# A GELU feed-forward block: all of x through DMA transposes on SyncE's queue, the plain loads on ScalarE's

## The chip, the core and the metric

The kernel runs on one core of a Trainium2 chip. A core has TensorE (PE: matrix products, with its own weight loads), VectorE (DVE), ScalarE (ACT), GpSimd (POOL) and SyncE (SP), which only issues DMAs and waits here. SyncE, ScalarE and GpSimd each have a queue from which DMAs are issued; one set of 16 DMA engines carries them out. The metric is the device time of one execution in microseconds. All times in the text count from the first instruction of the profiled execution.

## What is computed

```python
B, S, D, F = 1, 2048, 448, 1792           # bfloat16
h = jnp.einsum("bsd,df->bsf", x, w1) + b1
h = gelu(h)                               # tanh form
return jnp.einsum("bsf,fd->bsd", h, w2) + b2
```

Both products contract over the leading axis of what sits on the 128 partitions. So the first needs x with D on the partitions, that is x transposed; the second needs h with F on the partitions, which is how the first product writes it.

## The kernel before

**Tiling.** S = 2048 is cut into four chunks of 512 columns (c = 0 to 3). F = 1792 is 14 tiles of 128 (ft). D = 448 is covered by four slots of 128 rows that begin at rows 0, 128, 256 and 320 (k = 0 to 3; slots 2 and 3 overlap by 64 rows). A tile of the first product is therefore three full matmuls and one half, with 64 rows. Halves of neighbouring tiles run side by side.

**Order on TensorE.** Layer 1 of chunks 0 and 1, layer 2 of chunk 0, layer 1 of chunk 2, and so on; the order of the eight PSUM banks is fixed by hand (`jobs`, `number`). A chunk of layer 1 is two blocks: tiles 0 to 7, then 8 to 13. The first block of chunk 0 is written apart (`opening_block`): it runs k = 0 over all eight tiles, then k = 1 over all eight, then waits for k = 2 and 3 of w1 and does the rest. The second block waits for `sem_w1r`, the rest of w1's columns. ScalarE applies bias and GELU to each finished tile (L298), VectorE adds b2 to each output tile (L319), and SyncE stores it.

**The loads before.** SyncE issues all but one, in this order: chunk 0 of x as it lies in memory, in two halves (`xn_sb`, L142 and L143); the four k pieces of w1's first eight column tiles, 256 KB each (L120); the rest of w1's columns in two DMAs, 576 and 192 KB (L121 and L124); chunk 1 of x by four DMA transposes (L134), each of which brings 512 rows by 128 columns, 128 KB; w2 in two pieces of 784 KB (L128); b2 spread over the partitions (L148); chunks 2 and 3 of x by eight DMA transposes. GpSimd loads b1 (L164) after it has made the identity matrix.

**Chunk 0 before.** TensorE first runs NWARM = 11 matmuls on zeros (L170). Then it transposes chunk 0 against the identity (16 matmuls, L178) into PSUM; VectorE copies k = 0 and 1 to `xT_sb` (two casts, L310), ScalarE k = 2 and 3 (two casts, L291). b1 is transposed the same way (L187). The opening block waits for those copies: two of VectorE before the first matmul, b1 before the fourth, ScalarE's before the sixth and eighth.

```python
waits = {0: (sem_xTd, 2), 3: (sem_b1, 1), 5: (sem_xTa, 1), 7: (sem_xTa, 2)}
for k in (0, 1):
    pe.wait_ge(sem_w1[k], 16)
    for n, ft in enumerate(fts):
        if k == 0 and n in waits:
            pe.wait_ge(*waits[n])
        full(0, ft, k, k == 0, False)
```

Because chunk 0 is loaded with four neighbouring rows on one partition, its rows come out in another order, and its stores use a view of the output that puts them back (`out0_view`).

Of the kernel before, what the change touches and what calls it, by code (L numbers as in the profile page):

```python
# [7 lines left out]
BF16 = mybir.dt.bfloat16  # L8
# [3 lines left out]
def bass_standalone__dense_activation_gelu__prompt_kernel(  # L12
# [20 lines left out]

    KROW = [0, 128, 256, 320]
    NKT = len(KROW)

    WCUT = 8 * P
# [5 lines left out]
    W2_PIECES = [(0, 7), (7, 14)]  # L43
    NB = 8

    NWARM = 11
    WN = 256

    OCUT = 256
# [21 lines left out]
    with ExitStack() as es:  # L71
        sb = lambda n, s, d: es.enter_context(nc.sbuf_tensor(n, s, d))
        xT_sb = sb("xT_sb", [P, NKT, S], BF16)
        w1_sb = sb("wi_sb", [P, NKT, F], BF16)
        w2_sb = sb("wo_sb", [P, NFT, D], BF16)
        xn_sb = sb("xn_sb", [P, STC, D], BF16)
# [15 lines left out]
        sem_xn = [S_(f"sem_xn{i}") for i in range(2)]  # L92
# [4 lines left out]
        sem_xtp = S_("sem_xtp")  # L97
        sem_xTd = S_("sem_xTd")
        sem_xTa = S_("sem_xTa")
        sem_b1T = S_("sem_b1T")  # L100
        sem_b1 = S_("sem_b1")
        sem_l1 = S_("sem_l1")
# [4 lines left out]

        block = es.enter_context(nc.Block())


        x0_view = x2[0:SC, :].rearrange("(p t) d -> p t d", t=STC)
        out0_view = out2[0:SC, :].rearrange("(p t) d -> p t d", t=STC)

        def out_dram(j):
            return out0_view[:, j, :] if j < STC else out2[j * P:(j + 1) * P, :]

        def load_w1(eng):
            with nc.allow_non_contiguous_dma(reason="w1 column pieces"):
                for k, r in enumerate(KROW):
                    eng.dma_start(w1_sb[:, k, 0:WCUT], w1[r:r + P, 0:WCUT]).then_inc(sem_w1[k], 16)  # L120
                eng.dma_start(  # L121
                    w1_sb[:, 0:3, WCUT:F], w1[0:3 * P, WCUT:F].rearrange("(k p) f -> p k f", p=P)
                ).then_inc(sem_w1r, 16)
                eng.dma_start(w1_sb[:, 3, WCUT:F], w1[KROW[3]:D, WCUT:F]).then_inc(sem_w1r, 16)  # L124

        def load_w2(eng, i):
            a, b = W2_PIECES[i]
            eng.dma_start(  # L128
                w2_sb[:, a:b, :], w2[a * P:b * P, :].rearrange("(ft p) d -> p ft d", p=P)
            ).then_inc(sem_w2[i], 16)  # L130

        def load_xT(eng, c):
            for k, d0 in enumerate(KROW):
                eng.dma_start(  # L134
                    xT_sb[:, k, c * SC:(c + 1) * SC],
                    x2[c * SC:(c + 1) * SC, d0:d0 + P],
                    transpose=True,
                ).then_inc(sem_x[c], 16)

        @block.sync  # L140
        def _(sp):
            sp.dma_start(xn_sb[:, 0:2, :], x0_view[:, 0:2, :]).then_inc(sem_xn[0], 16)  # L142
            sp.dma_start(xn_sb[:, 2:4, :], x0_view[:, 2:4, :]).then_inc(sem_xn[1], 16)  # L143
            load_w1(sp)
            load_xT(sp, 1)
            for i in range(len(W2_PIECES)):
                load_w2(sp, i)
            sp.dma_start(b2_bc[:, :], b2.partition_broadcast(P)).then_inc(sem_b2, 16)  # L148
            for c in range(2, NSC):
                load_xT(sp, c)  # L150
# [16 lines left out]
        def _(pe):  # L167
            pe.wait_ge(sem_zero, 1)
            for _i in range(NWARM):
                pe.matmul(ps[0][:, 0:WN], lhsT=zeros[:, 0:P], rhs=zeros[:, :], start=True, stop=True)  # L170
            pe.wait_ge(sem_id, 2)

            for h in range(2):
                pe.wait_ge(sem_xn[h], 16)
                for k, d0 in enumerate(KROW):
                    for t in range(2):
                        col = (k % 2) * 2 * P + t * P
                        mm = pe.matmul(  # L178
                            ps[4 + 2 * h + k // 2][:, col:col + P],
                            lhsT=xn_sb[:, 2 * h + t, d0:d0 + P],  # L180
                            rhs=ident[:, :],
                            start=True, stop=True,
                        )
                    if k % 2:
                        mm.then_inc(sem_xtp, 1)
            pe.wait_ge(sem_b1n, 16)
            pe.matmul(  # L187
                ps[3][:, 0:NFT], lhsT=b1n_sb[:, :], rhs=ident[0:NFT, 0:NFT], start=True, stop=True
            ).then_inc(sem_b1T, 1)

            def free(kind, i):
                n = number[kind, i] - NB
                if n >= 0:
# [22 lines left out]
            def opening_block(first, second):  # L216

                fts = first + second
                waits = {0: (sem_xTd, 2), 3: (sem_b1, 1), 5: (sem_xTa, 1), 7: (sem_xTa, 2)}
                for k in (0, 1):  # L220
                    pe.wait_ge(sem_w1[k], 16)
                    for n, ft in enumerate(fts):
                        if k == 0 and n in waits:
                            pe.wait_ge(*waits[n])
                        full(0, ft, k, k == 0, False)
                pe.wait_ge(sem_w1[2], 16)
                pe.wait_ge(sem_w1[3], 16)
                for n, ft in enumerate(first):
                    full(0, ft, SLOTS[n % 2][2], False, False)
                for n, ft in enumerate(first):  # L230
                    half(0, ft, *HALVES[n % 2], False, True).then_inc(sem_l1, 1)
# [52 lines left out]

        @block.scalar
        def _(act):
            act.wait_ge(sem_zero, 1)
            act.activation(act_junk[:, :], zeros[:, 0:8], ACT.Gelu_apprx_tanh)  # L288
            for h in range(2):
# [12 lines left out]
            act.wait_ge(sem_osb, len(outs))  # L302
            act.dma_start(out_dram(NST - 1), out_sb[:, NST - 1, :]).then_inc(sem_od, 16)

        @block.vector
        def _(dve):
            dve.memset(zeros[:, :], 0.0).then_inc(sem_zero, 1)  # L307
            for h in range(2):
                dve.wait_ge(sem_xtp, 2 * h + 1)
                dve.tensor_copy(  # L310
                    xT_sb[:, 0:2, h * 256:(h + 1) * 256],
                    ps[4 + 2 * h][:, :].rearrange("p (k t) -> p k t", k=2),
                ).then_inc(sem_xTd, 1)
            dve.wait_ge(sem_b1T, 1)
            dve.tensor_copy(b1_f[:, :], ps[3][:, 0:NFT]).then_inc(sem_b1, 1)  # L315
# [35 lines left out]
```

## Time and profile before

| | |
|---|---|
| median of three runs | 97.1 us (96.87 to 99.33) |
| the profiled execution | 96.71 us |
| its span, first to last instruction | 94.9 us |
| TensorE busy | 90.8 us, 96% of the span |
| ScalarE busy | 35.8 us, 38% |
| VectorE busy | 11.8 us, 12% |
| first GELU of a real tile (L298) | 10.67 us |
| first store of an output tile (L153) | 31.35 us |
| granted clock of TensorE | 1.000 |

The page gives busy time by engine, the chain of waits that ended last, and the costliest groups of instructions. The DMA issues come with the time from issue to landing:

```profile
wo_sb<-in_w_dram SPq DMA_DIRECT2D x2, 784.0 KB, 7.0
wi_sb<-in_w_dram SPq DMA_DIRECT2D x4, 256.0 KB, 4.7
wi_sb<-in_w_dram SPq DMA_DIRECT2D x1, 576.0 KB, 6.3
xn_sb<-in_x_dram SPq DMA_DIRECT2D x2, 224.0 KB, 2.6
wi_sb<-in_w_dram SPq DMA_DIRECT2D x1, 192.0 KB, 6.3
xT_sb<-in_x_dram SPq DMA_TRANSPOSE x12, 4.4
```

Each line reads: what is written from what, the issuing queue, the operation, how many, the size of one, and the median time to landing in microseconds. `wi_sb` is w1, `wo_sb` is w2. A busy TensorE is not one at its peak, since its matmuls are pipelined and their ends are modelled; where the chain runs along TensorE without a break, the end moves one for one with what starts that stretch.

### The profile page before, as it was taken

What the parts mean: (1) busy time and instruction counts of PE and PEld (TensorE: products, weight loads), DVE (VectorE), ACT (ScalarE), POOL (GpSimd) and SP (SyncE); (2) the same over time, 40 slices, a digit from 0 to 9 for tenths busy, and PEclk for the clock granted to TensorE, in tenths of its full rate; (3) what the DMA queues carried; (4) which work ended last, traced back from release to release, by engine and by line L of the source; (5) the groups of instructions that cost most, each with busy time, mean ns of one, the idle gap of its engine ahead of it and who ended that gap; (6) DMA issues with size and microseconds to landing.
All of it is one profiled execution on the core that took longest, in us unless ns stands there. A gap on an engine that the chain in (4) does not pass through costs nothing.

```text
span 94.9 us, 1157 instructions
## 1 busy us (share of the span) xinstructions
PE 90.8 (96%) x490; PEld 44.1 (46%) x490; DVE 11.8 (12%) x21; ACT 35.8 (38%) x60; POOL 1.3 (1%) x7
## 2 busy tenths in 40 slices
PE   5989999999999999999999999999999999999990
PEld 3744343434345555434445545434435555555670
DVE  0230000000000222200000222200000222222130
ACT  6130599969395000059486000049577000000000
POOL 5000000000000000000000000000000000000000
DMA  2999989997520111100000111010000110111111
GB/s 48 303 289 342 211 204 368 205 111 137 94 52 0 48 48 48 33 22 0 0 3 0 48 48 43 8 52 0 0 0 0 48 42 13 41 48 55 48 48 48
DMA packets 12245, 7.50 MB, mean 79 GB/s; under 512 B 6992, under 2 KB 11728, under 8 KB 12240
## 3 DMA queue, kind: packets, MB, share of 16 engines
q1 hardware_dynamic: 12064, 7.31, 32.4%
q10 hardware_dynamic: 144, 0.11, 0.4%
q8 instruction: 4, 0.07, 0.3%
q0 software_dynamic: 32, 0.00, 0.0%
q14 instruction: 1, 0.01, 0.0%
HBM read 4.02 MB, written 1.84 MB: 62 GB/s over the span
## 4 chain that ended last, share of the span: by engine, by line
PE 95%; DVE 1%; issue 0%
PE ps L274 45%; PE ps L198 39%; PE ps L206 7%; PE ps L170 3%; PE ps L178 1%; DVE xT_sb L310 1%; DVE out_sb L319 0%; DVE zeros L307 0%
## 5 line engine op out<-in xcount | busy, mean ns | idle before, releaser
L298 ACT ACTIVATE g_sb<-ps,bi_f 128x512 bf16<-128x512 f32 x56 | 33.1, 706 | 33.9 <-PE ps L206 33.9
L274 PE MATMUL ps<-wo_sb,g_sb 128*128 128x448 bf16 (+2 forms) x238 | 42.9, 341 | 0.0
L198 PE MATMUL ps<-xT_sb,wi_sb 128*128 128x512 bf16 x168 | 38.1, 379 | 0.4 <-DVE xT_sb L310 0.4
L274 PEld LDWEIGHTS ps<-wo_sb,g_sb 128*128 128x128 bf16 x238 | 23.1, 98 | 19.7
L198 PEld LDWEIGHTS ps<-xT_sb,wi_sb 128*128 128x128 bf16 x168 | 15.7, 98 | 21.5 <-issue 3.4
L319 DVE TENSOR_TENSOR out_sb<-ps,bo_bc 128x448 bf16<-128x448 f32 (+2 forms) x17 | 10.2, 597 | 76.9 <-PE ps L274 76.9
L206 PE MATMUL ps<-xT_sb,wi_sb 64*128 64x512 bf16 x56 | 7.4, 379 | 0.0
L206 PEld LDWEIGHTS ps<-xT_sb,wi_sb 64*128 64x128 bf16 x56 | 2.1, 94 | 4.8 <-issue 3.4
L170 PE MATMUL ps<-zeros 128*128 128x256 bf16 x11 | 2.5, 419 | 1.1 <-DVE zeros L307 1.1
L170 PEld LDWEIGHTS ps<-zeros 128*128 128x128 bf16 x11 | 1.5, 145 | 1.6 <-DVE zeros L307 1.1
L291 ACT CAST xT_sb<-ps 128x512 bf16<-128x512 f32 x2 | 1.2, 585 | 2.4 <-PE ps L178 2.4
L310 DVE CAST xT_sb<-ps 128x512 bf16<-128x512 f32 x2 | 1.4, 692 | 3.2 <-PE ps L178 3.2
L178 PE MATMUL ps<-ident,xn_sb 128*128 128x128 bf16 x16 | 1.8, 300 | 0.0
L178 PEld LDWEIGHTS ps<-ident,xn_sb 128*128 128x128 bf16 x16 | 1.6, 142 | 0.3 <-issue 0.3
L288 ACT ACT_TABLE_LOAD x1 | 1.3, 1283 | 0.7 <-PEq L336 0.7
L164 POOL DMA_DIRECT2D bin_sb<-in_b_dram x1 | 0.6, 647 | 0.2 <-issue 0.2
L160 POOL TENSOR_SCALAR_AFFINE_SELECT ident<-ident 128x128 bf16<-128x128 bf16 x1 | 0.3, 287 | 0.2 <-POOL ident L158 0.2
L307 DVE MEMSET zeros<- 128x128 uint32 x1 | 0.2, 165 | 0.8 <-PEq L336 0.8
L288 ACT ACTIVATE act_junk<-zeros 128x8 bf16<-128x8 bf16 x1 | 0.2, 208 | 0.0
L158 POOL MEMSET ident<- 128x128 bf16 x1 | 0.2, 204 | 0.3 <-POOLq L336 0.3
L187 PE MATMUL ps<-ident,bin_sb 14*128 14x14 bf16 x1 | 0.2, 177 | 0.0
L315 DVE COPY bi_f<-ps 128x14 f32<-128x14 f32 x1 | 0.2, 162 | 0.0
(5 smaller groups left out, 0.5 us busy)
## 6 DMA issues: line engine op xcount, KB each, us to landing
out_dram<-out_sb SPq DMA_DIRECT2D x15, 112.0 KB, 1.7
wo_sb<-in_w_dram SPq DMA_DIRECT2D x2, 784.0 KB, 7.0
wi_sb<-in_w_dram SPq DMA_DIRECT2D x4, 256.0 KB, 4.7
wi_sb<-in_w_dram SPq DMA_DIRECT2D x1, 576.0 KB, 6.3
xn_sb<-in_x_dram SPq DMA_DIRECT2D x2, 224.0 KB, 2.6
wi_sb<-in_w_dram SPq DMA_DIRECT2D x1, 192.0 KB, 6.3
xT_sb<-in_x_dram SPq DMA_TRANSPOSE x12, 4.4
bo_bc<-in_b_dram SPq DMA_DIRECT2D x1, 112.0 KB, 7.6
```

What stands on the lines that cost most here:

```text
L160: pool.affine_select(out=ident[:, :], in_=ident[:, :], compare_op=ALU.not_equal, fill=1.0, base=0, pattern=[[-1, P]], channel_multiplier=1 ...
L164: pool.dma_start(b1n_sb[:, :], b1.rearrange("(c p) -> c p", p=P)).then_inc(sem_b1n, 16)
L170: pe.matmul(ps[0][:, 0:WN], lhsT=zeros[:, 0:P], rhs=zeros[:, :], start=True, stop=True)
L178: mm = pe.matmul(ps[4 + 2 * h + k // 2][:, col:col + P], lhsT=xn_sb[:, 2 * h + t, d0:d0 + P], rhs=ident[:, :], start=True, stop=True,)
L198: return pe.matmul(bank("g", order.index((c, ft)))[:, :], lhsT=w1_sb[:, k, ft * P:(ft + 1) * P], rhs=xT_sb[:, k, c * SC:(c + 1) * SC], sta ...
L206: return pe.matmul(bank("g", order.index((c, ft)))[:, :], lhsT=w1_sb[lo:lo + HALF, k, ft * P:(ft + 1) * P], rhs=xT_sb[lo:lo + HALF, k, c * ...
L274: mm = pe.matmul(bank("o", n)[:, 0:c1 - c0], lhsT=g_sb[:, ft, j * P:(j + 1) * P], rhs=w2_sb[:, ft, c0:c1], start=(ft == 0), stop=(ft == NF ...
L288: act.activation(act_junk[:, :], zeros[:, 0:8], ACT.Gelu_apprx_tanh)
L291: act.copy(xT_sb[:, 2:4, h * 256:(h + 1) * 256], ps[5 + 2 * h][:, :].rearrange("p (k t) -> p k t", k=2),).then_inc(sem_xTa, 1)
L298: act.activation(g_sb[:, ft, c * SC:(c + 1) * SC], bank("g", i)[:, :], ACT.Gelu_apprx_tanh, bias=b1_f[:, ft:ft + 1], scale=1.0,).then_inc( ...
L310: dve.tensor_copy(xT_sb[:, 0:2, h * 256:(h + 1) * 256], ps[4 + 2 * h][:, :].rearrange("p (k t) -> p k t", k=2),).then_inc(sem_xTd, 1)
L319: dve.tensor_tensor(out=out_sb[:, j, c0:c1], in0=bank("o", n)[:, 0:c1 - c0], in1=b2_bc[:, c0:c1], op=ALU.add,).then_inc(sem_osb, 1)
```

## The change

Chunk 0 of x now also comes by four DMA transposes, one per k, each with a semaphore of its own (`sem_x0[k]`). SyncE issues nothing but the sixteen transposes of x, chunk after chunk, and then the stores. ScalarE's queue takes the plain loads, ahead of ScalarE's first activation: the four pieces of w1, its rest, w2 and b2. TensorE's transposes of chunk 0, their four copies, `xn_sb` and the changed row order of chunk 0 go. NWARM is 17. The transposition of b1 stands between the second and the third matmul of the opening block, and its result is awaited before the eighth. The waits for k = 2 and 3 cover both x and w1.

```diff
-    NWARM = 11
+    NWARM = 17
...
+        sem_x0 = [S_(f"sem_x0_{k}") for k in range(NKT)]
...
-        def load_xT(eng, c):
-            for k, d0 in enumerate(KROW):
-                eng.dma_start(
-                    xT_sb[:, k, c * SC:(c + 1) * SC],
-                    x2[c * SC:(c + 1) * SC, d0:d0 + P],
-                    transpose=True,
-                ).then_inc(sem_x[c], 16)
+        def load_xT(eng, c, k):
+            eng.dma_start(
+                xT_sb[:, k, c * SC:(c + 1) * SC],
+                x2[c * SC:(c + 1) * SC, KROW[k]:KROW[k] + P],
+                transpose=True,
+            ).then_inc(sem_x[c] if c else sem_x0[k], 16)
...
         def _(sp):
-            sp.dma_start(xn_sb[:, 0:2, :], x0_view[:, 0:2, :]).then_inc(sem_xn[0], 16)
-            sp.dma_start(xn_sb[:, 2:4, :], x0_view[:, 2:4, :]).then_inc(sem_xn[1], 16)
-            load_w1(sp)
-            load_xT(sp, 1)
-            for i in range(len(W2_PIECES)):
-                load_w2(sp, i)
-            sp.dma_start(b2_bc[:, :], b2.partition_broadcast(P)).then_inc(sem_b2, 16)
-            for c in range(2, NSC):
-                load_xT(sp, c)
+            for c in range(NSC):
+                for k in range(NKT):
+                    load_xT(sp, c, k)
...
                 for k in (0, 1):
+                    pe.wait_ge(sem_x0[k], 16)
                     pe.wait_ge(sem_w1[k], 16)
                     for n, ft in enumerate(fts):
-                        if k == 0 and n in waits:
-                            pe.wait_ge(*waits[n])
+                        if k == 0 and n == 2:
+                            pe.wait_ge(sem_id, 2)
+                            pe.wait_ge(sem_b1n, 16)
+                            pe.matmul(
+                                ps[NB - 1][:, 0:NFT], lhsT=b1n_sb[:, :], rhs=ident[0:NFT, 0:NFT],
+                                start=True, stop=True,
+                            ).then_inc(sem_b1T, 1)
+                        if k == 0 and n == NB - 1:
+                            pe.wait_ge(sem_b1, 1)
                         full(0, ft, k, k == 0, False)
-                pe.wait_ge(sem_w1[2], 16)
-                pe.wait_ge(sem_w1[3], 16)
+                for k in (2, 3):
+                    pe.wait_ge(sem_x0[k], 16)
+                    pe.wait_ge(sem_w1[k], 16)
...
         def _(act):
+            for k in range(NKT):
+                load_w1(act, k)
+            load_w1_rest(act)
+            for i in range(len(W2_PIECES)):
+                load_w2(act, i)
+            act.dma_start(b2_bc[:, :], b2.partition_broadcast(P)).then_inc(sem_b2, 16)
             act.wait_ge(sem_zero, 1)
             act.activation(act_junk[:, :], zeros[:, 0:8], ACT.Gelu_apprx_tanh)
-            for h in range(2):
-                act.wait_ge(sem_xtp, 2 * h + 2)
-                act.copy(
-                    xT_sb[:, 2:4, h * 256:(h + 1) * 256],
-                    ps[5 + 2 * h][:, :].rearrange("p (k t) -> p k t", k=2),
-                ).then_inc(sem_xTa, 1)
```

`load_w1(eng, k)` and `load_w1_rest(eng)` are the two parts of the former `load_w1`, with the same DMAs.

More of the change, by code (lines that the diff above doesn't have):

```diff
@@ L75, in bass_standalone__dense_activation_gelu__prompt_kernel @@
         w2_sb = sb("wo_sb", [P, NFT, D], BF16)
-        xn_sb = sb("xn_sb", [P, STC, D], BF16)
         ident = sb("ident", [P, P], BF16)
@@ L91, in bass_standalone__dense_activation_gelu__prompt_kernel @@
         sem_b2 = S_("sem_b2")
-        sem_xn = [S_(f"sem_xn{i}") for i in range(2)]
+        sem_x0 = [S_(f"sem_x0_{k}") for k in range(NKT)]
         sem_b1n = S_("sem_b1n")
@@ L96, in bass_standalone__dense_activation_gelu__prompt_kernel @@
         sem_id = S_("sem_id")
-        sem_xtp = S_("sem_xtp")
-        sem_xTd = S_("sem_xTd")
-        sem_xTa = S_("sem_xTa")
         sem_b1T = S_("sem_b1T")
@@ L108, in bass_standalone__dense_activation_gelu__prompt_kernel, with load_w1, load_w1_rest @@
         block = es.enter_context(nc.Block())
-        x0_view = x2[0:SC, :].rearrange("(p t) d -> p t d", t=STC)
-        out0_view = out2[0:SC, :].rearrange("(p t) d -> p t d", t=STC)
         def out_dram(j):
-            return out0_view[:, j, :] if j < STC else out2[j * P:(j + 1) * P, :]
-        def load_w1(eng):
+            return out2[j * P:(j + 1) * P, :]
+        def load_w1(eng, k):
             with nc.allow_non_contiguous_dma(reason="w1 column pieces"):
-                for k, r in enumerate(KROW):
-                    eng.dma_start(w1_sb[:, k, 0:WCUT], w1[r:r + P, 0:WCUT]).then_inc(sem_w1[k], 16)
+                eng.dma_start(
+                    w1_sb[:, k, 0:WCUT], w1[KROW[k]:KROW[k] + P, 0:WCUT]
+                ).then_inc(sem_w1[k], 16)
+        def load_w1_rest(eng):
+            with nc.allow_non_contiguous_dma(reason="w1 column pieces"):
                 eng.dma_start(
@@ L130, in load_w2 @@
             ).then_inc(sem_w2[i], 16)
-        def load_xT(eng, c):
-            for k, d0 in enumerate(KROW):
-                eng.dma_start(
-                    xT_sb[:, k, c * SC:(c + 1) * SC],
-                    x2[c * SC:(c + 1) * SC, d0:d0 + P],
-                    transpose=True,
-                ).then_inc(sem_x[c], 16)
+        def load_xT(eng, c, k):
+            eng.dma_start(
+                xT_sb[:, k, c * SC:(c + 1) * SC],
+                x2[c * SC:(c + 1) * SC, KROW[k]:KROW[k] + P],
+                transpose=True,
+            ).then_inc(sem_x[c] if c else sem_x0[k], 16)
         @block.sync
         def _(sp):
-            sp.dma_start(xn_sb[:, 0:2, :], x0_view[:, 0:2, :]).then_inc(sem_xn[0], 16)
-            sp.dma_start(xn_sb[:, 2:4, :], x0_view[:, 2:4, :]).then_inc(sem_xn[1], 16)
-            load_w1(sp)
-            load_xT(sp, 1)
-            for i in range(len(W2_PIECES)):
-                load_w2(sp, i)
-            sp.dma_start(b2_bc[:, :], b2.partition_broadcast(P)).then_inc(sem_b2, 16)
-            for c in range(2, NSC):
-                load_xT(sp, c)
+            for c in range(NSC):
+                for k in range(NKT):
+                    load_xT(sp, c, k)
             for j in range(NST - 1):
@@ L170, in _ @@
                 pe.matmul(ps[0][:, 0:WN], lhsT=zeros[:, 0:P], rhs=zeros[:, :], start=True, stop=True)
-            pe.wait_ge(sem_id, 2)
-            for h in range(2):
[L174 to L189, printed above, removed]
             def free(kind, i):
@@ L218, in opening_block @@
                 fts = first + second
-                waits = {0: (sem_xTd, 2), 3: (sem_b1, 1), 5: (sem_xTa, 1), 7: (sem_xTa, 2)}
                 for k in (0, 1):
+                    pe.wait_ge(sem_x0[k], 16)
                     pe.wait_ge(sem_w1[k], 16)
                     for n, ft in enumerate(fts):
-                        if k == 0 and n in waits:
-                            pe.wait_ge(*waits[n])
+                        if k == 0 and n == 2:
[7 more added lines that the diff above has]
+                            pe.wait_ge(sem_b1, 1)
                         full(0, ft, k, k == 0, False)
-                pe.wait_ge(sem_w1[2], 16)
-                pe.wait_ge(sem_w1[3], 16)
+                for k in (2, 3):
+                    pe.wait_ge(sem_x0[k], 16)
+                    pe.wait_ge(sem_w1[k], 16)
                 for n, ft in enumerate(first):
@@ L286, in _ @@
         def _(act):
+            for k in range(NKT):
[4 more added lines that the diff above has]
+            act.dma_start(b2_bc[:, :], b2.partition_broadcast(P)).then_inc(sem_b2, 16)
             act.wait_ge(sem_zero, 1)
             act.activation(act_junk[:, :], zeros[:, 0:8], ACT.Gelu_apprx_tanh)
-            for h in range(2):
-                act.wait_ge(sem_xtp, 2 * h + 2)
-                act.copy(
-                    xT_sb[:, 2:4, h * 256:(h + 1) * 256],
-                    ps[5 + 2 * h][:, :].rearrange("p (k t) -> p k t", k=2),
-                ).then_inc(sem_xTa, 1)
             act.wait_ge(sem_b1, 1)
@@ L307, in _ @@
             dve.memset(zeros[:, :], 0.0).then_inc(sem_zero, 1)
[L308 to L313, printed above, removed]
             dve.wait_ge(sem_b1T, 1)
-            dve.tensor_copy(b1_f[:, :], ps[3][:, 0:NFT]).then_inc(sem_b1, 1)
+            dve.tensor_copy(b1_f[:, :], ps[NB - 1][:, 0:NFT]).then_inc(sem_b1, 1)
             dve.wait_ge(sem_b2, 16)
```

## Prediction

> **What bounds the kernel now.** I read the chain of waits first, by engine and then in order of time. By engine:
>
> ```profile
> PE 95%; DVE 1%; issue 0%
> ```
>
> TensorE carries the chain; only its start holds anything that is not matrix work. The pieces in order of time (start, length, what) show where a change to the first loads can act:
>
> ```profile
> 1.06 2.53 PE ps L170 x11
> 3.59 1.32 PE ps L178 x12
> ...
> 4.93 0.70 DVE xT_sb L310
> ...
> 5.77 4.48 PE ps L198 x20
> ```
>
> Warm-up matmuls, the transposes of chunk 0, one copy out of PSUM, and at 5.77 us the first real matmul. From there PE runs unbroken to 92.36. So the new time is the old one plus the shift of the last point at which PE waits for data. That point is somewhere in the first blocks of chunk 0, so I read SyncE's own timeline next (start, length of all):
>
> ```profile
> 1.67 1.85 SPq L120 DMA_DIRECT2D wi_sb<-in_w_dram  x4
> 3.56 0.43 SPq L121 DMA_DIRECT2D wi_sb<-in_w_dram  x1
> 4.03 0.49 SPq L124 DMA_DIRECT2D wi_sb<-in_w_dram  x1
> 4.56 5.83 SPq L134 DMA_TRANSPOSE xT_sb<-in_x_dram  x4
> ```
>
> A plain load costs the issuing queue 0.43 to 0.49 us, a DMA transpose about three times that. More important is the order: the transposes of chunk 1 stand behind all of w1. The answer for line L134 between 20.7 and 26 us, where nothing else is queued, gives the bare cost (min/median/max ns, then landing in us from the start of issue):
>
> ```profile
> L134 SPq DMA_TRANSPOSE xT_sb<-in_x_dram x4: 1262/1262/1263, 20.6 to 24.6; - x4
> ...
> DMA to landing us min/median/max: 3.2/3.5/3.6
> ```
>
> With 0.05 between them, one transpose leaves every 1.31 us. The DMA views of two stretches, 3.3 to 8.5 (almost only w1) and 21 to 22 (only transposes), give the two rates:
>
> ```profile
> DMA packets 958, 1.56 MB, mean 301 GB/s; under 512 B 114, under 2 KB 450, under 8 KB 958
> ```
> ```profile
> DMA packets 1036, 0.25 MB, mean 249 GB/s; under 512 B 1036, under 2 KB 1036, under 8 KB 1036
> ```
>
> Two transposes a microsecond: 0.5 us of all 16 engines each, in 512 packets of 256 B, 32 per engine. A 256 KB piece of w1 (128 rows, 8 packets per engine) takes 0.87 us at 301 GB/s, 0.11 a packet. Last, the table by stage around 20 us (PE, PEld, DVE, ACT, POOL, clock, DMA share, GB/s) and, for 18.9 to 20.9, the DMA queues:
>
> ```profile
> 19.40:20.90 1.50, 1.50 (x12) 0.55 (x12) 0.00 (x0) 1.02 (x2) 0.00 (x0) 1.00 1.64 16
> ```
> ```profile
> q1 hardware_dynamic: 560, 0.14, 148.7%
> q8 instruction: 1, 0.02, 3.7%
> ```
>
> Transposes were queued, yet traffic fell to 16 GB/s for 1.5 us: one packet of another queue (16 KB of instructions) was on one engine. I read it as transposes advancing at the pace of the engine that is most held up. It is the one place in this trace where a transpose meets a second queue; all plain loads share the transposes' queue now.
>
> **The change, step by step.** Times are on the profiled execution's axis; it took 96.71 us, 1.8 beyond its span and 0.4 under the median of 97.1. I add shifts to the median.
>
> *Removed:* the xn loads (448 KB, 1.5 us of the engines at 301 GB/s), 16 PE transposes (1.77 us), four casts (0.69 and 0.58 each), and the wait on the last cast. All lie ahead of 5.77.
>
> *Warm-ups, 11 to 17.* Eleven run from 1.06 to 3.46: 0.218 each. Seventeen end at 4.77; no real matmul starts earlier. These 256-column matmuls take as long as the 512-column ones later, so PE starts at half pace; for the first few real ones that is a cost between 0 and 0.2 us, since the pace had changed by 5.77 after a similar stretch of work. I take 0, as the idle stretch is short.
>
> *Chunk 0 by transposes.* SyncE's first slot is 0.75. Undisturbed, T0 lands 3.2 to 3.6 later; but the first transpose in this trace took 1.92 to issue, not 1.26, which may be a cost of any first one. So T0 lands between 4.0 and 5.0. w1's first piece leaves ScalarE at about 0.75 (its first instruction now starts at 0.74); xn's loads landed 2.6 after issue, so it is there by about 3.7. Opening: 4.9 instead of 5.77. The 16 matmuls of k = 0 and 1 take 3.5 (0.22 each), to 8.4. T3 leaves at 4.7 to 5.3 and lands at 7.9 to 8.9; w1's fourth piece landed at 8.3 (3.08 plus 5.2) behind xn's 448 KB and now shares with 512 KB of transposes, 64 KB more, 0.2: 8.5. I take 8.6 for the k = 2 and 3 part, against 9.3: 0.7 gained. Its 2.75 us then end at 11.4, where the second block now begins at 12.0.
>
> *Bias and ScalarE.* The transposition of b1 moves behind the second real matmul, at 5.3; its load landed at 4.8 (1.67 plus 3.1), so 0.5 covers it, and beyond that PE stalls one for one. DVE's copy (0.16) has five matmuls, 1.1 us. ScalarE now issues nine loads: 1.85, 0.43, 0.49, 1.19 and 0.60 with gaps, to 5.5; then the table load (1.28) and the dummy (0.21), to 7.0. Behind them waits the first GELU, due at about 9.9 (10.67 less 0.8). That covers 2.9, also a hold-up like the 2.1 beyond 1.26 that one transpose of L134 met behind w2. Free on both sides.
>
> *The rest of w1 (L121, L124).* The second block waits for it (sem_w1r). It landed at 9.8 and 10.3, ahead of every transpose. Now transposes run beside it from about 2.4, one each 1.31, and nothing holds those of chunk 1 back. Time t of its landing: 10.3, less 1.5 for xn, plus 0.5 for each of (t - 2.4)/1.31 transposes. That gives t = 12.75. If a transpose took only half of its 0.5 away from plain loads, it is 10.3; if it took 0.6, 14.2; 0.7, 16.1. I take 0.5, which is measured; the ends stay for the range. The second block then starts at 12.7 instead of 12.0: **+0.7 us**.
>
> *Later.* T7 leaves at 10.6, lands by 14.2; chunk 1 is due at 12.7 + 3.4 = 16.1, cover 1.9. w2 (1.6 MB, 5.2 us, beside eight transposes, 4 us) is there by 22, due at 27.9 + 0.7. T15 lands by 25, due at 38. SyncE's 16 issues end at 22.4, its first store was at 31.35. The stores of chunk 0 change their row order, not their size: nothing. If any cover went, the overshoot would be paid one for one.
>
> Sum: -0.9 at the opening, +0.2 at k = 3, +1.4 at w1's rest: 97.1 + 0.7 = **97.8**.
>
> **Rivals.**
>
> *The rest of w1 arrives in time.* If transposes mostly use gaps of the plain stream, the 0.7 gained at k = 3 stays: 96.4. For it: 3.3 to 8.5 ran at 301 GB/s, and 16 to 17 us at 378, so there is slack. Against it: the DMA engines are 90% and more busy there.
>
> *Starved weights (the other side).* Each transpose halts all 16 engines until the slowest has caught up, and w1's rest pays for it. Place: the wait ahead of the second block. Price: the landing above, 14.2 at 0.6 us per transpose, 16.1 at 0.7; slower by 2% from 14.0, about 0.59 on. Middle: 15.1, +3.1, 100.2. For it: 16 GB/s around 20 us. Against: there one packet blocked for 1.2 us; w1's take 0.11.
>
> *Turns of a whole piece.* If an engine alternates between the queues by large portions, a transpose of two such portions waits for two pieces of w1: 2 x (0.25 + 0.87) = 2.2 us each. T2 and T3 meet w1's rest and w2 at similar portions: T3 ends near 11, lands near 11.5, so the k = 3 part starts 2.2 late, and chunk 1, at 2 us each, adds about 0.4: 99.7. [...] No run here shows two busy hardware queues, so it stays open. The same with single packets (32 turns of 0.015 + 0.11, 4 us for T0, less for the next as the packets get smaller) puts T3 near 12.5, landed at 13.0: +3.7, 100.8. Against both: the pieces may well alternate in transposes' favour.
>
> **How the numbers follow.** Forecast (96.8 to 99.0 of its own) 0.42; w1's rest in time 0.13; starved weights 0.20; turns, of either size, 0.25. Faster by 2%, about what a measurement of this kernel can tell from no change, would need 95.2: the second block 1.9 earlier, at 10.1, but 4.8 + 3.5 + 2.75 = 11.05 is its floor. I leave 0.03 for an error in that floor. Within 2% (up to 99.0): forecast and the first rival, 0.52. Slower: 0.45. The range runs from just under the first rival, 96.3, to 100.8, where the second kind of turns ends; more than that, the upper starved cases, is left out.
>
> **What would show it.** T0 landing after 5.5, or transposes of chunk 0 that take far more than 1.31 to issue, would break the opening. A gap on PE between k = 1 and k = 2 of 2 us or more with a late transpose shows turns; a gap ahead of the second block that ends with a w1 landing shows the starved or the forecast case, told apart by its length (1.3 against 3 and more). No gap at all, and PE starting near 4.9, is the first rival. A late first GELU or a gap behind the second matmul would show a cover that failed.

## The result, and the profile after

The changed kernel takes 102.75 us (median of four runs, 101.98 to 103.63) against 97.35 us of the kernel before (four runs): a ratio of 1.057, 95% interval 1.053 to 1.061. The profiled execution took 103.31 us, its span is 101.5 us against 94.9. So 6.6 us of span have to be found. Ratios and intervals, here and below, leave out the executions of either kernel that took over 1.5% longer than its fastest, so that a ratio need not be that of the medians. In the changed kernel the transposes of x are line L129, the full matmuls of layer 1 L167, the halves L175, and T0 to T3 are the four transposes of chunk 0. Landings named below without a line are read from the trace's DMA completions.

The chain of waits by engine, which was TensorE's at 95%, and one piece of it in order of time (start, length, what):

```profile
PE 83%; DMA 9%; SPq 4%; issue 1%; DVE 0%
```
```profile
4.86 9.13 DMA xT_sb<-in_x_dram
```

One transpose, T3, issued at 4.86 us and landed 9.13 us later, is now the longest piece of the start. TensorE's own timeline (start, length of all; in brackets the idle time before and what ended it) shows what that does:

```profile
5.05 0.61 PE L167 MATMUL ps<-xT_sb,wi_sb 128*128 128x512 bf16 x2 [0.18 <-DMA xT_sb<-in_x_dram]
6.99 0.16 PE L195 MATMUL ps<-ident,bin_sb 14*128 14x14 bf16 x1 [1.33 <-DMA bin_sb<-in_b_dram]
7.09 1.47 PE L167 MATMUL ps<-xT_sb,wi_sb 128*128 128x512 bf16 x6
8.91 1.90 PE L167 MATMUL ps<-xT_sb,wi_sb 128*128 128x512 bf16 x8 [0.36 <-DMA xT_sb<-in_x_dram]
14.23 1.02 PE L167 MATMUL ps<-xT_sb,wi_sb 128*128 128x512 bf16 x4 [3.42 <-DMA xT_sb<-in_x_dram]
15.19 1.88 PE L175 MATMUL ps<-xT_sb,wi_sb 64*128 64x512 bf16 x8
```

The opening starts at 5.05, earlier than the 5.77 of before. Then TensorE waits three times: for b1, for T1, and 3.4 us for T3. The k = 2 part starts at 14.23, where it was 9.2 before: 5.0 us. The eight halves behind it then take 1.88 us, where they took 1.04 before:

```profile
10.18 1.04 PE L206 MATMUL ps<-xT_sb,wi_sb 64*128 64x512 bf16 x8
```

The table by stage (busy PE, PEld, DVE, ACT, POOL, then granted clock, DMA share, GB/s) tells why:

```profile
10.80:14.20 3.40, 0.01 (x1) 0.00 (x0) 0.00 (x0) 0.29 (x2) 0.00 (x0) 1.00 1.13 317
15.20:18.60 3.40, 3.27 (x12) 1.01 (x13) 0.00 (x0) 2.71 (x5) 0.00 (x0) 0.50 1.24 278
```

3.4 us with one matmul are followed by 3.4 us at a granted clock of 0.50, which costs about 1.7 us. From there on the chain is the old one, shifted. One piece of it (start, length, what), before and after:

```profile
15.53 3.99 PE ps L198 x18
```
```profile
22.18 3.99 PE ps L167 x18
```

That is 6.65 later, 5.0 from the late data and 1.65 from the clock. Nothing further is lost; layer 2 of chunk 0 and all that follows keeps its length.

The four transposes of chunk 0, as line L129 shows them (min/median/max of the issue in ns, then landing in us):

```profile
L129 SPq DMA_TRANSPOSE xT_sb<-in_x_dram x4: 1188/1385/1881, 0.8 to 4.9; - x4
...
DMA to landing us min/median/max: 4.3/7.8/9.1
```

They leave on time and land late: at 5.0, 8.9, 12.1 and 14.0 us. What they met shows in the DMA queues between 12.5 and 16.5 us, where SyncE's queue (q1) holds transposes and ScalarE's (q10) w2:

```profile
q10 hardware_dynamic: 1259, 1.11, 79.9%
q1 hardware_dynamic: 1254, 0.30, 34.4%
```

1,259 packets of one queue, 1,254 of the other, at nearly four times the bytes (1.11 MB against 0.30): as if every engine took one packet from each in turn.

### The profile page after: what moved, and what is told of

Read it like the earlier page. It is cut to its first block, busy times and chain, and to the rows that moved or that the text cites. A ratio compares the mean times of both kernels' runs of the same rounds, so it can differ in the third digit from the quotient of the medians.

```text
span 101.5 us, 1131 instructions
## 1 busy us (share of the span) xinstructions
PE 92.0 (91%) x474; PEld 43.4 (43%) x480; DVE 10.5 (10%) x19; ACT 34.7 (34%) x58; POOL 1.3 (1%) x7
## 4 chain that ended last, share of the span: by engine, by line
PE 83%; DMA 9%; SPq 4%; issue 1%; DVE 0%
PE ps L251 42%; PE ps L167 33%; DMA xT_sb<-in_x_dram 9%; PE ps L175 8%; SPq L129 4%; DVE out_sb L290 0%
## 5 line engine op out<-in xcount | busy, mean ns | idle before, releaser
L167 PE MATMUL ps<-xT_sb,wi_sb 128*128 128x512 bf16 x162 | 38.3, 384 | 4.6 <-DMA xT_sb<-in_x_dram 4.0
L167 PEld LDWEIGHTS ps<-xT_sb,wi_sb 128*128 128x128 bf16 x168 | 15.6, 99 | 26.7 <-issue 8.8
L290 DVE TENSOR_TENSOR out_sb<-ps,bo_bc 128x448 bf16<-128x448 f32 (+2 forms) x17 | 10.2, 597 | 81.9 <-PE ps L251 81.9
L175 PE MATMUL ps<-xT_sb,wi_sb 64*128 64x512 bf16 x56 | 8.3, 414 | 0.0
L159 PE MATMUL ps<-zeros 128*128 128x256 bf16 x17 | 3.8, 419 | 1.1 <-DVE zeros L284 1.1
L175 PEld LDWEIGHTS ps<-xT_sb,wi_sb 64*128 64x128 bf16 x56 | 2.2, 98 | 5.1 <-issue 3.9
L159 PEld LDWEIGHTS ps<-zeros 128*128 128x128 bf16 x17 | 2.4, 146 | 2.0 <-DVE zeros L284 1.1
```

What stands on the lines that cost most here:

```text
L167: return pe.matmul(bank("g", order.index((c, ft)))[:, :], lhsT=w1_sb[:, k, ft * P:(ft + 1) * P], rhs=xT_sb[:, k, c * SC:(c + 1) * SC], sta ...
L175: return pe.matmul(bank("g", order.index((c, ft)))[:, :], lhsT=w1_sb[lo:lo + HALF, k, ft * P:(ft + 1) * P], rhs=xT_sb[lo:lo + HALF, k, c * ...
L290: dve.tensor_tensor(out=out_sb[:, j, c0:c1], in0=bank("o", n)[:, 0:c1 - c0], in1=b2_bc[:, c0:c1], op=ALU.add,).then_inc(sem_osb, 1)
```

## The experiments

Theory "turns": with both queues filled, every engine takes one packet of each in turn, however long it is. A transpose is 32 packets per engine, so beside plain loads it waits for 32 of theirs, and it was sent out with all of w1 and w2 beside it. Rivals: chunk 1 takes the engine time of w1's rest (a term of the forecast); transposes are slow at the start of a kernel whatever runs beside them; GpSimd's third queue causes it; the queues share by bytes. A second question is what the half pace adds and where it comes from.

**1. Filling the wait ahead of k = 2** (fill_gap).

```diff
+                for _i in range(28):
+                    pe.matmul(bank("g", order.index((0, fts[0])))[:, 0:WN],
+                              lhsT=zeros[:, 0:P], rhs=zeros[:, :], start=False, stop=False)
                 for k in (2, 3):
```

> The changed kernel with 28 matmuls on zeros (256 columns, adding zero to the first tile) between k = 1 and k = 2 of the opening block; nothing else differs. Theory 'turns': the last transpose of chunk 0 still lands near 14 us, since no load is touched; the fill (28 x 0.107 = 3.0 us) lies inside the 3.4 us wait, so TensorE is not idle long enough to fall to half pace, and the 3.4 us at half pace from 15.2 us (1.7 us lost) go: about 101 us where the changed kernel shows a clock of 0.983. Rival 'the half pace is not from the gap': same time as the changed kernel or up to 3 us more.

Measured: 102.46 us, ratio 1.054 (1.045 to 1.062). T3 landed at 14.05 as expected, and nothing ran at half pace after it. But a half pace came earlier, and the fill then began at 12.0 and reached past T3. One row of the table by stage:

```profile
9.00:10.00 1.00, 1.00 (x4) 0.41 (x3) 0.00 (x0) 0.11 (x1) 0.00 (x0) 0.50 1.28 296
```

It follows the first wait, for b1 from 5.7 to 7.2. So this run is inconclusive on the size; it showed that this shorter wait, too, can be followed by half pace. Run 8 fills all waits of the opening.

**2. w2 and b2 behind chunk 1 on SyncE's queue** (w2_behind_c1).

```diff
             for c in range(NSC):
                 for k in range(NKT):
                     load_xT(sp, c, k)
+                if c == 1:
+                    for i in range(len(W2_PIECES)):
+                        load_w2(sp, i)
+                    sp.dma_start(b2_bc[:, :], b2.partition_broadcast(P)).then_inc(sem_b2, 16)
```

> The changed kernel with w2 and b2 back on SyncE's queue, behind chunk 1's transposes; ScalarE's queue keeps all of w1. Theory 'turns' (each engine takes one packet of either queue in turn, 32 packets of a transpose against as many plain packets as are queued): only w1's 64 packets per engine stand beside chunk 0, so T0 and T1 are slow and T2 and T3 are not; T3 lands near 10.9 instead of 14.0, the k = 2 part starts near 11 and the time is about 98.7. Rival 'chunk 1 takes the share of w1's rest': nothing is won, w1's rest lands as late or later than its 12.3 us and the time stays above 101. Rival 'transposes are slow at the start whatever runs beside them': T3 stays near 14.

Measured: 100.73 us, 1.039 (1.033 to 1.046). T2 landed at 11.7 and T3 right behind at 12.2, instead of 12.1 and 14.0. The direction is that of "turns", though T3 is 1.3 us later than expected; the time is 2 us above its number, because of TensorE:

```profile
5.58 1.03 PE L171 MATMUL ps<-xT_sb,wi_sb 128*128 128x512 bf16 x2 [0.71 <-DMA xT_sb<-in_x_dram]
...
8.10 6.46 PE L171 MATMUL ps<-xT_sb,wi_sb 128*128 128x512 bf16 x18
```

Eighteen matmuls in 6.5 us: most of them are 0.43 apart, not 0.22. This half pace did not begin with a wait: the first two matmuls already take 1.03 us together, where the changed kernel took 0.61, so the pace had not yet risen from that of the warm-ups (17 of 256 columns in 3.81 us, 0.22 each). TensorE then waited for b1 from 6.6 to 8.0, and the pace rose only at 13.0; T3 had landed by then, and nothing waited for it. The granted clock reads 1.000 for this run and 1.00 in every microsecond from 2 to 19 us, also from 8 to 13 with about four matmuls a microsecond; so here a clock of 1.000 alone does not show full pace.

**3. Only the first four pieces of w1 beside chunk 0** (rest_held): as 2, and

```diff
             for k in range(NKT):
                 load_w1(act, k)
+            act.wait_ge(sem_zero, 1)
+            act.activation(act_junk[:, :], zeros[:, 0:8], ACT.Gelu_apprx_tanh)
+            act.wait_ge(sem_x0[NKT - 1], 16)
             load_w1_rest(act)
```

> As the run with w2 behind chunk 1, and ScalarE also holds w1's rest until chunk 0 has landed; only the four first pieces of w1 (32 packets per engine) stand beside chunk 0. Theory 'turns': T0 near 5, the others at SyncE's pace of issue; T3 near 9, the k = 2 part near 9, w1's rest lands 3.5 us after its issue, near 12.5; 97.4 us. Rival 'slow at the start': T3 stays near 14, time above 101. Rival 'chunk 1 takes the share': w1's rest, now issued behind chunk 1's first transposes, lands after 14.5, time above 99.5.

Measured: 101.49 us, 1.045 (1.039 to 1.051). T0 to T3 landed at 5.1, 9.0, 9.4 and 9.8: T1 with the last of the four pieces (8.9), T2 and T3 right behind. That is "turns" to within 1 us, and 4 us earlier than in the changed kernel with the same transposes on the same queue: the rival "slow at the start" is out. The time was not won, and TensorE's timeline shows two other waits in its place:

```profile
8.02 6.71 PE L171 MATMUL ps<-xT_sb,wi_sb 128*128 128x512 bf16 x18
...
16.79 2.76 PE L171 MATMUL ps<-xT_sb,wi_sb 128*128 128x512 bf16 x12 [0.33 <-DMA wi_sb<-in_w_dram]
```

Half pace from the first matmul on, as in run 2, until 13.4, and then w1's rest: issued from 9.9, it landed at 16.7, 7 us after instead of 3.5, with chunk 1's transposes beside it. Here the expectation of "turns" was wrong and that of the rival "chunk 1 takes the share" came true (after 14.5, time above 99.5): the overlap hurt plain loads in this run, too.

**4. Everything on one queue** (one_queue): SyncE issues T0, piece 0 of w1, T1, piece 1, and so on, then w1's rest, chunk 1, w2, b2, chunks 2 and 3.

> All loads on SyncE's queue in the order T0, first piece of w1, T1, second piece, T2, third, T3, fourth, rest of w1, chunk 1, w2, b2, chunks 2 and 3. Theory 'turns': with one queue there is nothing to alternate with; T3 leaves near 6.1 and lands near 9.6, the fourth piece near 10, w1's rest near 11.9: the k = 2 part starts 0.7 later than in the kernel before, 98 us. Rival 'a transpose and a plain load slow each other on any queue': T3 lands after 12, time above 100.

Measured: 100.14 us, 1.025 (1.017 to 1.033), above the 98 expected; the profiled execution took 98.94, its span is 97.1. The transposes and the first matmul behind the opening's last wait:

```profile
DMA to landing us min/median/max: 3.1/3.2/3.6
```
```profile
11.47 1.02 PE L175 MATMUL ps<-xT_sb,wi_sb 128*128 128x512 bf16 x4 [1.79 <-DMA wi_sb<-in_w_dram]
```

T3 landed at 9.5, as expected, 3.3 after its issue; so the transposes, issued in turn with plain loads on one queue, took 3.1 to 3.6 us to land here, where they took 4.3 to 9.1 in the changed kernel. The fourth piece of w1 landed at 11.3 instead of 10, and the k = 2 part waits for that. Why the first three pieces took 3.2 to 3.3 us each and the fourth 3.9 stays open.

**5. The transposes alone** (bare_transposes): ScalarE waits for `sem_x0[3]` ahead of all its loads.

> The changed kernel, but ScalarE issues its plain loads only when chunk 0 has landed, so that the four transposes run with nothing beside them but b1's small load. Theory 'turns': they land at SyncE's pace of issue, 3.3 us after it: near 4.1, 5.4, 6.7 and 8.0 us, where they landed at 5.0, 8.9, 12.1 and 14.0 beside the plain loads. Rival 'transposes are slow at the start whatever runs beside them': the fourth after 10. The kernel as a whole is slow in both (w1 leaves near 8, the opening starts near 10.5, then waits for w1's rest): 103 us or more.

Measured: 105.27 us (one run). Line L129, the four of chunk 0:

```profile
L129 SPq DMA_TRANSPOSE xT_sb<-in_x_dram x4: 1195/1248/1261, 0.8 to 4.6; - x4
...
DMA to landing us min/median/max: 2.7/2.8/2.8
```

They land at 3.4, 4.7, 6.1 and 7.4. So T3's landing at 14.0 in the changed kernel is no price of transposing by DMA: 6.6 us of it come from what stands beside it.

**6. Chunk 1 held until w1's rest has landed** (hold_chunk1): SyncE waits for `sem_w1r` ahead of chunk 1.

> The changed kernel, but SyncE issues chunk 1 only when the rest of w1 has landed. The prediction's term 'chunk 1 takes the share of w1's rest': w1's rest lands 1.4 us or more earlier than its 12.3 us and the wait of TensorE shrinks by as much. Theory 'turns': T3 is ahead of chunk 1 in its own queue, so it still lands near 14, w1's rest near 12, and the time stays within 1 us of the changed kernel's.

Measured: 103.83 us (one run). T3 landed at 14.5 and w1's rest at 13.0, so nothing came earlier for holding chunk 1 back. The rival "chunk 1 takes the share of w1's rest" falls for the changed kernel, where chunk 1 stands behind T3 in any case: its first transpose landed at 15.7, w1's rest at 12.3. Where chunk 0 is through earlier, as in run 3 (w1's rest 7 us after its issue), the rival holds.

**7. b1 on ScalarE's queue, ahead of w1** (b1_scalar).

> The changed kernel, but b1 is loaded first on ScalarE's queue instead of GpSimd's. Its landing (6.9 us in the changed kernel) held TensorE from 5.5 to 7.0 behind the second matmul, and traffic fell to 153 GB/s between 5 and 6. Theory 'turns': b1 lands near 3, k = 0 runs through from 5.1, k = 1 still waits for T1 near 8.5 and k = 2 for T3 near 13.5: within 1 us of the changed kernel. Rival 'the third queue causes the dip and with it the late transposes': traffic from 5 to 6 stays near 280 GB/s, T1 lands by 7.5, T3 by 12.5, time 1.5 us or more lower.

Measured: 104.05 us (102.2 to 104.27, no interval). TensorE's timeline:

```profile
5.21 1.47 PE L166 MATMUL ps<-xT_sb,wi_sb 128*128 128x512 bf16 x6
10.21 2.85 PE L166 MATMUL ps<-xT_sb,wi_sb 128*128 128x512 bf16 x8 [3.53 <-DMA xT_sb<-in_x_dram]
15.10 1.87 PE L166 MATMUL ps<-xT_sb,wi_sb 128*128 128x512 bf16 x4 [2.04 <-DMA xT_sb<-in_x_dram]
```

b1 no longer holds anything, k = 0 runs through, and yet T1 (10.2) and T3 (14.9) are as late as before, with traffic at 116 GB/s between 5 and 7 us. The third queue is not the cause.

**8. All waits of the opening filled** (fill_all): 12 matmuls on zeros ahead of b1's transposition, 4 ahead of k = 1, 28 ahead of k = 2.

> The changed kernel with matmuls on zeros in all three waits of the opening block (12 before b1's, 4 before k = 1, 28 before k = 2), so that TensorE is hardly idle before T3 lands. No load is touched. Theory 'turns' with the clock: T3 lands near 14 as before, the k = 2 part starts near 14.3 and all of it runs at 0.22 per matmul: span near 99.9 instead of 101.5, time near 101. What is then left over the kernel before, some 4 to 5 us, is the late data alone. Rival 'the half pace comes whatever TensorE does in the waits': matmuls at 0.43 after 14 us again, time as the changed kernel's.

Measured: 102.13 us, 1.051 (1.047 to 1.055), span 100.3.

```profile
11.61 3.22 PE L214 MATMUL ps<-zeros 128*128 128x256 bf16 x28
14.66 1.03 PE L168 MATMUL ps<-xT_sb,wi_sb 128*128 128x512 bf16 x4
```

The first two matmuls were still at half pace; from 6.8 us on there is none, with no load touched: what the changed kernel had from 15.2 came from the idle time. T3 landed at 14.0, the fill reached 0.6 past it, and the start of the k = 2 part, 5.4 later than before the change, is now the whole of the 5.4 us of span. Over the medians the clock is worth less than in the profiled executions (102.13 against 102.75, and intervals that overlap): one of the changed kernel's own executions had a clock of 1.000 and 102.18 us (which, as run 2 shows, does not rule out half pace).

**9. Short packets for w1's rest** (short_packets): its large part in three strips of 256 columns.

```diff
-                eng.dma_start(
-                    w1_sb[:, 0:3, WCUT:F], w1[0:3 * P, WCUT:F].rearrange("(k p) f -> p k f", p=P)
-                ).then_inc(sem_w1r, 16)
+                for a in range(WCUT, F, 256):
+                    eng.dma_start(
+                        w1_sb[:, 0:3, a:a + 256],
+                        w1[0:3 * P, a:a + 256].rearrange("(k p) f -> p k f", p=P),
+                    ).then_inc(sem_w1r, 16)
```

> The changed kernel, but the large part of w1's rest is loaded in three strips of 256 columns: the same bytes in packets of 512 B, 72 per engine instead of 24 of 1536 B. If an engine alternates packet by packet, a transpose beside it waits for less: T2 lands near 10.8 instead of 12.1 and T3 near 12 instead of 14.0; time 1.5 us or more lower than the changed kernel's. Rival 'the two queues share by bytes, or the transposes are late because of the volume of the plain loads': T2 and T3 land as before, within 0.5 us, and the time does not move.

Measured: 101.50 us, 1.045 (1.036 to 1.054). T2 landed at 11.6, 2.3 after T1 instead of 3.3; T3 at 13.8, hardly earlier. For T3 this is what the rival expected. The expectation had overlooked that with three times as many packets w1's rest still stands beside T3 (it landed at 13.9), where w2's packets of 896 B stood in the changed kernel. T2 alone is a hint for "packet by packet", no more.

**10. Long packets for w2** (long_packets): `"(ft p) d -> p ft d"` becomes `"(p ft) d -> p ft d"`.

> The changed kernel, but w2 is read with seven neighbouring rows of 896 B on one partition, in packets of 6272 B, 16 per engine instead of 112 of 896 B, the same bytes; w2's rows so stand on other partitions than h's, and the second product is a different one. The plain packets beside T2 and T3 are 0.3 us long instead of 0.05. Packet by packet: T2 lands near 15 and T3 near 16 (12.1 and 14.0 in the changed kernel). Shared by bytes: both as before, within 0.5 us.

Measured: 110.99 us (one run). T2 landed at 16.6 and T3 at 20.6, with the same bytes beside them. The DMA queues between 11.5 and 14.5 us:

```profile
q10 hardware_dynamic: 205, 1.09, 95.7%
q1 hardware_dynamic: 203, 0.05, 8.2%
```

205 packets against 203, while one queue moves 1.09 MB and the other 0.05. So in this run the queues shared by packets and not by bytes. That a turn was one packet shows in the starts: a packet of 6272 B took 0.24 us in this trace and one of a transpose 0.02, and on both queues the starts repeat every 0.25. The changed kernel's trace shows it in the order of the starts between 12.5 and 16.5 us: 32 starts in a row, as many as two for each of the 16 engines, take 0.052 us (median), 83% of such stretches hold exactly 16 of either queue, and 88% of the starts are of the same queue as the one 32 before. T3 is later than the 16 us expected from turns: from 14.5 to 20 us traffic was at 129 GB/s on average, with w2's queue on 22.9% of the engines' time. That fits the reading that a transpose advances at the pace of the engine that is most held up; no run tried that alone.

**11. The rest on SyncE's queue, waits filled** (rest_sp_fill): b1 first on ScalarE's queue, then w1's four pieces; SyncE issues chunk 0, w1's rest, chunk 1, w2, b2, chunks 2 and 3; 14 matmuls on zeros ahead of k = 1.

> Beside chunk 0 only the four first pieces of w1 on ScalarE's queue (b1 ahead of them); w1's rest, chunk 1, w2 and b2 follow chunk 0 on SyncE's queue; 14 matmuls on zeros between k = 0 and k = 1 keep TensorE busy (18 warm-ups). Theory 'turns' with the clock: T0 near 5, T1 near 8.8 with w1's last piece, T2 and T3 right behind, by 9.9; k = 1 from 8.9 to 10.7 at full pace, k = 2 from 10.7 against 9.3 before, w1's rest by 12.5 without a wait: +1.4, 98.6 us. If the half pace seen in the run with w1's rest held (16 matmuls at 0.43 instead of 0.22) has another cause than the idle time from 5.8 to 7.9, it stays: 101 us or more.

Measured: 98.99 us, 1.018 (1.014 to 1.021).

```profile
9.93 2.76 PE L173 MATMUL ps<-xT_sb,wi_sb 128*128 128x512 bf16 x12 [0.86 <-DMA xT_sb<-in_x_dram]
```

Twelve matmuls without a break and at full pace: k = 1, and k = 2 right behind, at 11.7. The first two matmuls were at half pace (1.06 us for two), but with no wait for b1 the pace rose at 6.2 and not at 13, as in runs 2 and 3. T1 landed at 9.9 with w1's last piece, 1 us later than expected; everything left hangs on it.

**12. w1's third and fourth piece held until T1 has landed** (paced): as 11, and

```diff
-            for k in range(NKT):
+            for k in (0, 1):
                 load_w1(act, k)
             act.wait_ge(sem_zero, 1)
             act.activation(act_junk[:, :], zeros[:, 0:8], ACT.Gelu_apprx_tanh)
+            act.wait_ge(sem_x0[1], 16)
+            for k in (2, 3):
+                load_w1(act, k)
```

> As the run with w1's rest on SyncE's queue and filled waits, but ScalarE issues the third and fourth piece of w1 only when T1 has landed (fill: 4 before k = 1, 8 before k = 2). If an engine takes one packet of either queue in turn, T0 and T1 stand beside 16 plain packets per engine in all and not 32: T1 lands near 6.5 instead of 9.9, k = 1 ends near 8.6; the two held pieces, issued near 6.6, land beside T2 and T3 by 10; the k = 2 part starts near 10 against 11.7 there and 9.3 before the change: 97.9 us. If the transposes beside w1 are late for another reason than the number of plain packets beside them, T1 stays after 8.5 and the time at 99 or more.

Measured: 99.56 us, 1.027 (1.022 to 1.031). The transposes of chunk 0, and the wait that took their place:

```profile
DMA to landing us min/median/max: 2.7/3.6/4.1
```
```profile
12.06 1.02 PE L173 MATMUL ps<-xT_sb,wi_sb 128*128 128x512 bf16 x4 [2.34 <-DMA wi_sb<-in_w_dram]
```

T1 landed at 6.1 and T3 at 7.3 instead of 8.9 and 14.0: fewer plain packets beside them, earlier transposes. But the two held pieces landed at 9.7 and 11.9, beside w1's rest on the other queue. The expectation had not counted that overlap.

**13 and 14. w1's rest behind the held pieces on ScalarE's queue** (paced_rest), and with chunk 1 held as well until the fourth piece has landed (paced_rest_hold):

```diff
             for c in range(NSC):
+                if c == 1:
+                    sp.wait_ge(sem_w1[3], 16)
                 for k in range(NKT):
                     load_xT(sp, c, k)
-                if c == 0:
-                    load_w1_rest(sp)
```

> As the paced run, but w1's rest follows the two held pieces on ScalarE's queue instead of standing on SyncE's (fill of 4 before k = 2). There the held pieces landed at 9.7 and 11.9 us, with w1's rest beside them on the other queue, though T3 was there at 7.3. Packet by packet: the held pieces, issued near 6.2, now meet only chunk 1's short packets: they land by 9.3, the k = 2 part starts near 9.3 as in the kernel before, w1's rest lands by 12: 97.0 to 97.6 us, the kernel before's time. If chunk 1's transposes slow the held pieces as much as w1's rest did, the fourth piece lands after 11 and the time is 99 or more.

> As the run before it, but chunk 1 waits on SyncE's queue until the fourth piece of w1 has landed. Nothing stands beside the held pieces but T2 and T3: they land by 8.8, the k = 2 part starts at 8.8, w1's rest lands by 12; chunk 1, issued from 8.8, lands by 17 where it is due near 15.5: a new wait of 1 to 1.5 us, 97.5 to 98.5 us.

Measured: 100.03 us, 1.020 (1.013 to 1.027), and 97.97 us, 1.009 (1.005 to 1.012). In the first, the fourth piece landed at 10.9 and w1's rest at 14.9 beside chunk 1, so the second branch of its expectation holds, if narrowly (it said after 11, and 99 or more). In the second, TensorE's timeline:

```profile
10.01 1.02 PE L173 MATMUL ps<-xT_sb,wi_sb 128*128 128x512 bf16 x4 [0.56 <-DMA wi_sb<-in_w_dram]
...
13.44 2.76 PE L173 MATMUL ps<-xT_sb,wi_sb 128*128 128x512 bf16 x12 [0.46 <-DMA wi_sb<-in_w_dram]
```

The k = 2 part starts at 10.0 and the second block is 1.4 us late, as w1's rest landed at 13.4 and not by 12; the wait for chunk 1 that was expected did not come (landed 16.7, when TensorE was still in the second block). All sixteen transposes are still SyncE's and w1 is ScalarE's, yet of the 5.7% of the change 0.9% are left. No version was faster than the kernel before.

## Why the prediction was wrong

The forecast was 97.8 us in a range of 96.3 to 100.8; measured were 102.75. Step by step:

- *Opening at 4.9.* Right: 5.05. The warm-ups ended where the sum put them, and T0 landed at 5.0, the late end of what was allowed.
- *T3 at 7.9 to 8.9, the k = 2 part at 8.6.* This is the step that failed. T3 left at 4.86, as reckoned, but landed at 14.0. The step took the landing of a transpose with nothing beside it (3.2 to 3.6 us; the bare run shows 2.8) and charged T3 nothing for the plain loads beside it; it counted the company for w1's fourth piece alone, and by bytes: 64 KB more, 0.2 us. In the traces the engines shared by packets: 1,254 of SyncE's queue against 1,259 of ScalarE's in the changed kernel, 203 against 205 beside packets of 6272 B. In 256 B packets the transposes so had 34.4% of the engines' time beside 79.9% (packets of 896 B), and 8.2% beside 95.7% (6272 B). Taking the company away brought T3 to 9.8 with four pieces of w1 left, to 7.3 with two and 7.4 with none.
- *w1's fourth piece at 8.5* was right (8.3, as in the kernel before). It lost far less than T3, which landed at 14.0 against 7.4 in the bare run.
- *w1's rest at 12.75, as the wait that ends last.* The landing was about right (12.3), but by luck: the sum charged w1's rest for eight transposes, and three had landed by then. The place was wrong: TensorE came there at 18.7. Holding chunk 1 back did not bring the landing earlier, so the half microsecond per transpose did not act as reckoned here. Nor is the term empty: with chunk 0 through, w1's rest beside chunk 1 landed 7 us after its issue (run 3), and at 14.9 in run 13 against 13.4 with chunk 1 held in run 14. The rival built on the same term, starved weights, named a wait that the changed kernel does not have.
- *Half pace at 0, "as the idle stretch is short".* This was said of the first matmuls, and for them it was right in the profiled execution (0.61 us for two); in runs 2, 3, 8 and 11 they took 1.03 to 1.06. The forecast had no term for a pace that falls again. That is the second miss, 1.65 us in the profiled execution, and a consequence of the first: the wait for T3 became 3.4 us. A granted clock of 0.50 for 3.4 us followed, and filling the waits removed it. How long a wait has to be for that is not shown: in runs 1 and 6 the clock fell to 0.50 after waits of 1.6 and 1.7 us, while in run 12 it did not after one of 2.3 (four matmuls in 1.02 us behind it, clock 1.000). What triggers the fall stays open.
- *b1 covered by 0.5.* It landed at 6.9 instead of 4.8 and held TensorE 1.3 us, paid one for one as stated, but behind the later T1 this cost nothing in itself. In runs 2 and 3 this wait fell into a stretch in which the pace had not risen yet.
- *ScalarE free by 7.0.* Its queue backed up more than allowed for: b2's issue took 3.1 us and the table load began at 9.6. The first GELU was then due at 15.9, so the cover held only because the data were late.
- *The rival "turns".* What the runs showed, in its second form, single packets: T3 was put at 13.0 and the time at 100.8. It lacked the half pace and about 1 us of T3. The first form's sum, 99.7, takes a transpose as two large portions, each beside a whole piece of w1. No run shows such portions; the starts in run 10 and in the changed kernel show turns of one packet, 256 B against 6272 or 896 B. The chance given to "turns" of either size, 0.25, was too low: all that the forecast held against it, that the pieces "may well alternate in transposes' favour", rested on no row. The one place where the trace of before showed a transpose meeting another queue, 16 GB/s around 20 us, it used for starved weights alone.

What stays open: the traffic of the stretch from 5 to 7 us (162 GB/s in the changed kernel, 116 with b1 on ScalarE's queue, 283 before the change with almost only plain loads). One-for-one turns account for late transposes, but not by themselves for a slower sum of both: between 12.5 and 16.5 the same mixing ran at 354 GB/s. The reading that transposes stall all engines until the last one has caught up would fit both, but no run isolates it.

## What to carry to other kernels

Two hardware queues were not just two issuers here: they were interleaved packet by packet (1,254 against 1,259), and the transfer with the short packets lost (T3 landed 9.1 us after its issue, against 3.3 with all loads on one queue). When loads are moved to a second queue, count the packets per engine that each urgent transfer will meet there, and let what is not yet needed wait on a semaphore. And if a step is to wait for data, price the pace of TensorE behind it, too: here 1.6 us of waiting could be followed by half pace (run 1), and a clock of 1.000 did not rule it out (run 2), so read the spacing of the matmuls.

## What the runs showed that was not expected

- A DMA transpose of 128 KB landed 2.7 to 2.8 us after its issue with only b1's small load beside it (run 5), and, in chunk 0 of the changed kernel, up to 9.1 us after it beside a full plain queue (16.0 in run 10, with long packets there).
- In the changed kernel ScalarE's DMA issues stretched from 0.39 us (w1's first piece) to 3.1 (b2), the more loads stood ahead of them, and ScalarE's own work waited behind them until 9.6.
- Holding plain loads back brought the urgent transfers forward, at a price for the held ones: with two pieces of w1 held until T1 had landed, and w1's rest and w2 behind the transposes (run 12), chunk 0 was complete at 7.3 instead of 14.0 us, and w1's fourth piece at 11.9 instead of 8.3.
